# First pair's stores cut into transfers of one block row, with the planner's costs and priorities set anew

## The chip, the cores and the metric

The kernel runs on one core of a Trainium2 chip. The metric is device time in microseconds (us); before the change it was 748.63 us, the median of three runs (746.96 to 749.18).

## The reference

Eight batches of eight heads attend through 32 packed queries, and the result goes through a feed-forward layer with a GELU:

```python
def sm_attn(qq, kk, vv):                       # scale = 1/8
    s = scale * np.matmul(qq, kk.transpose(0, 1, 3, 2))
    a = np.exp(s - np.max(s, axis=-1, keepdims=True))
    a = a / (np.sum(a, axis=-1, keepdims=True) + 1e-09)
    return np.matmul(a, vv)

p_packed = sm_attn(p, k, v)                    # p: (8, 8, 32, 64); q, k, v: (8, 8, 576, 64)
out = sm_attn(q, p_packed, p_packed)           # (8, 8, 576, 64)
x = out.transpose(0, 2, 1, 3).reshape(4608, 512)
h = x @ w_in                                   # w_in: (512, 2048)
g = 0.5 * h * (1.0 + erf(h / np.sqrt(2.0)))
return g @ w_out                               # w_out: (2048, 512); result (4608, 512)
```

Everything is float32, and q, k and p are eight times larger than drawn.

## The kernel before

The batches go in four pairs. For each pair the attention ends in softmax weights `a2T` and packed values `pp`. The feed-forward layer of a pair is four units, one for each 512 columns of `w_in`; a unit has eight steps (`t8`), four for each batch of the pair, 32 steps a pair and 128 in all. In a unit `pp` is first multiplied by `w_in` (`wps`, L1118). A step then forms 128 hidden columns (`h`, L1184, or L1175 in the first unit), ScalarE takes the GELU into `graw` (L1206) and a rounded copy `g` (L1213), VectorE subtracts the copy from `graw` for the low part of `g` (L1215), and TensorE adds `g` times `w_out` into four output tiles `o` (L1236 to L1238, three products each; the third reads the low part). A ninth output tile of the unit, `o_edge`, takes the last 64 rows of both batches. VectorE adds the units' results into nine tiles `acc` of 128 rows by 512 (L1322), and after the fourth unit these are stored.

While a pair's steps run, the attention of the next pair runs beside them. `later_pair` (L1348) starts it when the step named in `LATER["from"]` comes up and the pair before has its scores. It loads p (L623), k and q (L563) and v (L612, L614). For pairs after the first, a k or q load is four transfers of 32 partitions, 144 KB each, and VectorE then transposes blocks (`kT`, `qT`, L581). The weights are decoded in the first pair (`wraw`, L1042 and L1046), kept in DRAM (`ws`, L1099) and read back as `w` in the later pairs (L1017). All transfers are issued by SyncE (SP), in one queue.

The first pair's rows lie in another order than the other pairs': an `acc` tile holds four blocks of 32 rows, and the rows of a block stand 18 apart in the output. So its store (L1337) writes through a view with the block outermost, `[4, 32, 512]`, or, for the tile that holds the end of one batch and the beginning of the other, two views with two blocks each. The other pairs store 128 rows that lie together (L1330).

The order of the instructions on each engine is written by a planner (`Order`), which runs the program twice: once without priorities, to get each operation's distance to the end (`tails_of`, with the factors `SLACK` and the offsets `EARLY` by kind and `SOONER` by name), and once with them, in which each engine and the transfer queue issue the ready operation of the highest priority. It reckons transfers with a number of issues and bytes: for each issue 0.5 us of the queue, and the bytes at one rate over one link (`issue`, L391 to L394). `MARGIN` and `DMA_MARGIN` are times by which it lets an operation begin later than what it reads is reckoned to be there, once the output steps have begun:

```python
if engine == DMA and self.steady:
    after += DMA_MARGIN
```

Here `engine` is that of the task's own operation just before (L332); an operation that waits for an event of another task has no such margin. While the first products are not there, TensorE is filled with products of zeros (`idle`, L1157). `FIRST["banks"]` says where the first pair's second scores are held in PSUM (L642), and `FIRST["turn"]` which engine copies the first pair's transposed k and q (L574).

Of the kernel before, what the change touches and what calls it, by code (L numbers as in the profile page):

```python
# [25 lines left out]
NB32 = S // 32  # L26
# [13 lines left out]
PE, ACT, DVE, POOL, DMA = "PE", "ACT", "DVE", "POOL", "DMA"  # L40
# [9 lines left out]


SLACK = {
    "batch0": 1.513,
    "batch1": 2.222,
    "attention": 2.432,
    "load0": 0.271,
    "load": 0.122,
    "w_in0": 3.279,
    "w_out0": 2.037,
    "w_in": 0.772,  # L60
    "w_out": 2.153,
    "packed_w_in": 1.479,
    "steps": 0.535,
}
EARLY = {
    "batch0": 15.0,
    "batch1": -9.3,
    "attention": 0.1,
    "load0": 0.7,
    "load": 21.2,  # L70
    "w_in0": 2.2,
    "w_out0": 6.9,
    "w_in": 0.2,
    "w_out": -8.0,
    "packed_w_in": -4.5,
    "steps": -3.6,
}

SOONER = {
    "0_0_0": 11.8,  # L80
    "0_0_1": 13.7,
    "0_1_0": -13.7,
    "0_1_1": -4.6,
    "0_2_0": -2.6,
    "0_3_0": -1.8,
    "0_4_0": -14.8,
    "0_5_0": 2.6,
    "chunk_0_0": -12.2,
    "chunk_0_1": 19.3,
    "chunk_1_0": -3.5,  # L90
    "chunk_1_1": -6.2,
    "softmax1": -18.6,
    "softmax1_0_0": 5.1,
    "softmax1_0_1": 20.8,
    "softmax1_1_0": -4.3,
    "softmax1_1_1": -36.8,
    "softmax2": -5.0,
    "softmax2_0_0": -11.8,
    "softmax2_0_1": -53.3,
    "softmax2_1_0": -17.3,  # L100
    "softmax2_1_1": -1.0,
    "wp_0_0": -19.7,
    "wp_0_1": -6.8,
    "wp_1_0": -5.1,
    "wp_1_1": -25.2,
}

MARGIN = 2.0

DMA_MARGIN = 3.0  # L110

STEP_MORE = 1.18

# [10 lines left out]
    "scores2": (21.8, 25.2),  # L124
    "softmax2": (27.3, 16.8, 34.3, 83.9),
    "weights2": (31.8, 53.8, 41.5, 53.2),
    "from": (2, 0, 2, 0),
    "groups1": ((0, 1, 2, 3),),
    "groups2": ((0, 1), (2, 3)),
}  # L130
# [19 lines left out]
    "groups2": ((0,), (1,), (2,), (3,)),  # L150
    "gpsimd": (1,),
    "copy": ('ACT', 'ACT', 'ACT', 'ACT'),
    "banks": (False, False, False, False),
    "small": (True, True, True, True),
    "together": True,

# [1 line left out]
        "decode": (0, 0, 0, 0, 0, 0, 0, 0), "rebias": (0, 0, 0, 0, 0, 0, 0, 0), "k": (0, 0, 0, 0), "q": (0, 0, 0, 0),  # L158
        "softmax1": (0, 0, 0, 0), "softmax2": (0, 0, 0, 0), "packed": (0, 0, 0, 0), "weights2": (0, 0, 0, 0),
    },  # L160
    "turn": {"k": ('DVE', 'ACT', 'ACT', 'ACT'), "q": ('ACT', 'DVE', 'ACT', 'ACT')},
}


# [98 lines left out]
class Order:  # L263
# [31 lines left out]
    def fire(self, event):  # L295
        if self.current:
            event.by = event.by | self.current.by
        event.count -= 1
        if event.count == 0:
            for fn in event.waiting:  # L300
                self.at(self.now, fn)

    def advance(self, task, value, engine):
# [16 lines left out]
        if isinstance(what, Op):  # L320
# [11 lines left out]
            if engine == DMA and self.steady:  # L332
                after += DMA_MARGIN
            first = 0 if self.dry else -self.tails[key] - SOONER.get(key, 0) - (SOONER.get(what.takes[0][1], 0) if what.takes else 0)
# [96 lines left out]
def packed_attention_gelu_ffn(ctx: ExitStack, tc: tile.TileContext, q, k, v, p, w_in, w_out, out):  # L431
# [12 lines left out]
    nc = tc.nc  # L444
# [14 lines left out]
    def plan(order):  # L459
# [801 lines left out]
        def output_steps():  # L1261
            for n in range(NU * 8):
                u, t8 = divmod(n, 8)
                j, c = divmod(t8, NC4)
                yield g_ready[n]
                if n % STEPS == LATER["from"][n // STEPS]:
                    fire(pair_started[n // STEPS])
                yield w_ready[u, 2 + c, 0]
                if order.dry:
                    yield from behind(n)  # L1270
                order.idle, order.steady = None, True
                g, w = gs.pop(n), wo[u, c]
                if c == 0:
                    ts = [None] * 4
                for i in range(4):
                    def product(*new, i=i):
                        cols = slice(i * P, (i + 1) * P)
                        three(new[0] if new else ts[i], (g[:, 0, cols], g[:, 1, cols]), w, c == 0, c == NC4 - 1)


                    new = () if c > 0 else (i,) if u > 0 else range(4) if i == 0 and FIRST["together"] else () if FIRST["together"] else (i,)
                    got = yield Op(
                        PE, 0.68, n, product, [(psum_o, f"o_{n}_{x}") for x in new], more=0 if i else STEP_MORE)
                    if new:
                        ts[i:i + len(new)] = got if len(new) > 1 else [got]
                    if c == NC4 - 1:
                        start(finish(u, i + 5 * j, ts[i], psum_o, n))
                gts.give(g)
                if j == 1 and c == NC4 - 1:
                    start(edge_output(u, n))  # L1290

        def edge_output(u, n):
            yield t4_ready[u]
            t = None
            for c in range(NC4):
                def product(*new):
                    g = t4[u, c]
                    three((new[0] if new else t)[:, 0], (g[:, 0], g[:, 1]), wo[u, c], c == 0, c == NC4 - 1)

                got = yield Op(PE, 0.68, n, product, [(wide, f"o_{u}_edge")] if c == 0 else [])  # L1300
                t = got if c == 0 else t
                t4s.give(t4.pop((u, c)))
                free_wo(u, c)
            yield from finish(u, 4, t, wide, n)
# [8 lines left out]
        def finish(u, i, t, ring_, n):  # L1313
            pr, f = divmod(u, NF)
            x = t[:, 0] if ring_ is wide else t
            if f == 0:
                acc[pr, i] = yield Op(ACT, 0.48, n, lambda a: nc.scalar.copy(a, x), [(accs, f"acc_{pr}_{i}")])
                ring_.give(t)
                fire(finished[u, i])
                return  # L1320
            a = acc[pr, i]
            yield Op(DVE, 0.6, n, lambda: nc.vector.tensor_tensor(a, x, a, ALU.add))  # L1322
            ring_.give(t)
            fire(finished[u, i])
            if f == NF - 1:
                r0 = pr * 2 * S + i * P

                def fn():
                    if pr:
                        nc.sync.dma_start(out[r0:r0 + P], a)  # L1330
                        return
                    for j in range(2):
                        rows = out[j * S:(j + 1) * S].rearrange("(x n) d -> n x d", n=NB32)
                        n0, n1 = max(4 * i - j * NB32, 0), min(4 * i + 4 - j * NB32, NB32)
                        if n0 < n1:
                            p0 = 32 * (n0 + j * NB32 - 4 * i)
                            nc.sync.dma_start(rows[n0:n1], a[p0:p0 + 32 * (n1 - n0)])  # L1337

                yield Op(DMA, (1 if pr or i != 4 else 2, 262e3), n, fn)
                fire(written[pr, i])  # L1340
                accs.give(a)

# [70 lines left out]
```

## Time and profile before

| what | value |
|---|---|
| median of three runs | 748.63 us |
| the profiled execution | 749.43 us |
| its span, first to last instruction | 747.7 us |
| mean granted clock of TensorE | 0.995 |
| TensorE busy | 729.9 us, 98% |
| VectorE, ScalarE, GpSimd busy | 392.7, 355.9, 149.7 us |
| transferred | 106.77 MB in 156049 packets, 143 GB/s over the span |

Busy time is the share of the span in which an engine's instructions run; a matmul's end is modelled. In the rows below PE is TensorE, DVE VectorE, ACT ScalarE, SPq the queue of SyncE, which issues the transfers. Lines of a timeline give the start, the time taken, engine, source line, operation, tiles (out<-in), shapes and count, and in brackets the idle time of the engine before, with what ended it.

### The profile page before, as it was taken

The page shows a single profiled execution, that of the slowest core. Times are in us where ns is not written, and L with a number is a line of the kernel's source. Part 1 is how long each engine was busy: PE and PEld are TensorE (multiplying, and loading weights), DVE is VectorE, ACT ScalarE, POOL GpSimd, SP SyncE. Part 2 cuts the span into 40 slices and gives each one's busy share as a digit, 9 for nine tenths or more (in the row PEclk, how much of TensorE's full clock was granted, in tenths as well). Part 3 has the DMA queues.
Part 4 walks back from the last instruction along what each step waited for, and adds up shares of the span by engine and source line. Part 5 has one row for each costly group of instructions (what it writes and reads, how often), then busy time and mean ns, then how long its engine had stood idle before and what let it go on. Part 6 is the DMA issues. An engine that isn't in the chain of part 4 may idle for free.

```text
span 747.7 us, 13236 instructions
## 1 busy us (share of the span) xinstructions
PE 729.9 (98%) x5313; PEld 588.6 (79%) x5313; DVE 392.7 (53%) x614; ACT 355.9 (48%) x601; POOL 149.7 (20%) x312
## 2 busy tenths in 40 slices
PE   8999999999999599999999999999999999999997
PEld 6677787787777478788777888788777888788886
DVE  5778858887783131652568341563458421333332
ACT  5788656856653233453445243363355243332331
POOL 2443444453411001101011110101011011101010
PEclk9999999999999999999999999999999999999999
DMA  9977997575516698332051999341241701303031
GB/s 303 370 257 124 250 205 227 157 250 199 170 59 198 102 181 218 40 130 83 23 179 59 276 167 198 76 117 67 64 167 59 240 1 59 112 29 113 1 112 71
DMA packets 156049, 106.77 MB, mean 143 GB/s; under 512 B 123732, under 2 KB 131924, under 8 KB 155988
## 3 DMA queue, kind: packets, MB, share of 16 engines
q1 hardware_dynamic: 155988, 105.93, 53.2%
q8 instruction: 42, 0.69, 0.4%
q14 instruction: 19, 0.16, 0.1%
HBM read 83.89 MB, written 22.02 MB: 142 GB/s over the span
## 4 chain that ended last, share of the span: by engine, by line
PE 87%; SPq 3%; DMA 3%; DVE 3%; ACT 2%; issue 1%; POOL 1%; ACTq 0%; DVEq 0%; POOLq 0%
PE h L1184 24%; PE o L1236 16%; PE o L1238 15%; PE o L1237 15%; PE wps L1118 4%; SPq L563 3%; PE o_edge L1236 2%; PE o_edge L1238 2%; PE o_edge L1237 2%; PE h L1175 2%; PE s L657 2%; DMA k<-in_k_dram 2%; DMA wraw<-in_moe_w_out_dram 1%; PE pp L799 1%; PE e1Tm L761 1%
## 5 line engine op out<-in xcount | busy, mean ns | idle before, releaser
L1184 PEld LDWEIGHTS h<-a2T,wp 128*128 128x128 f32 x1440 | 202.6, 188 | 14.7 <-issue 3.5
L1184 PE MATMUL h<-a2T,wp 128*128 128x288 f32 x1440 | 210.6, 295 | 0.4 <-DVE e L848 0.4
L1236 PE MATMUL o<-w,g 128*128 128x512 f32 x508 | 206.8, 407 | 2.0 <-DMA w<-ws 1.6
L1238 PE MATMUL o<-w,g 128*128 128x512 f32 x508 | 200.6, 395 | 8.1 <-DVE g L1215 8.1
L1206 ACT ACTIVATE graw<-h 128x576 f32<-128x576 f32 x127 | 82.8, 652 | 261.0 <-PE h L1184 241.4
L1237 PE MATMUL o<-w,g 128*128 128x512 f32 x508 | 199.5, 393 | 0.0
L1215 DVE TENSOR_TENSOR g<-graw,g 128x512 fp32r<-128x512 f32 x128 | 95.4, 746 | 195.4 <-ACT g L1213 195.2
L1226 POOL CAST t<-graw 128x64 fp32r<-128x64 f32 x128 | 35.2, 275 | 513.6 <-ACT graw L1206 393.1
L1236 PEld LDWEIGHTS o<-w,g 128*128 128x128 f32 x508 | 96.3, 190 | 44.1 <-issue 22.7
L1238 PEld LDWEIGHTS o<-w,g 128*128 128x128 f32 x508 | 96.1, 189 | 31.3 <-DVE g L1215 9.8
L1237 PEld LDWEIGHTS o<-w,g 128*128 128x128 f32 x508 | 96.1, 189 | 14.8
L1322 DVE TENSOR_TENSOR acc<-o,acc 128x512 f32<-128x512 f32 x96 | 63.4, 683 | 35.5 <-PE o L1238 35.5
L1213 ACT CAST g<-graw 128x512 fp32r<-128x512 f32 x128 | 79.4, 620 | 3.2
L1134 DVE TENSOR_TENSOR wp<-wps,wp 128x1024 fp32r<-128x1024 f32 x30 | 36.7, 1222 | 38.5 <-ACT wp L1129 38.5
L1129 ACT CAST wp<-wps 128x1024 fp32r<-128x1024 f32 x30 | 30.4, 1014 | 43.5 <-PE wps L1118 43.5
L1227 POOL TENSOR_TENSOR t<-graw,t 128x64 fp32r<-128x64 f32 x128 | 47.1, 368 | 10.2
L1118 PE MATMUL wps<-w,pp 64*32 64x512 f32 (+1 forms) x544 | 35.3, 576 | 0.0
L581 DVE STREAM_TRANSPOSE kT<-k 128x1152 f32<-128x1152 f32 x12 | 16.5, 1376 | 27.7 <-DMA k<-in_k_dram 27.6
L1157 PE MATMUL idle<-still 128*128 128x256 bf16 x201 | 27.2, 287 | 1.1 <-DVE still L455 1.1
L1088 POOL TENSOR_TENSOR wt<-wt 128x512 int32<-128x512 int32 x16 | 21.7, 1356 | 31.0 <-DVE wt L1066 25.4
L1080 POOL TENSOR_TENSOR w<-wt 128x512 int32<-128x512 int32 x16 | 22.7, 1423 | 22.4 <-DVE wt L1066 19.8
L1052 ACT ACTIVATE wt<-wraw 128x512 f32<-128x512 f32 x32 | 21.6, 675 | 9.8 <-DMA wraw<-in_moe_w_in_dram 6.1
(124 smaller groups left out, 668.6 us busy)
## 6 DMA issues: line engine op xcount, KB each, us to landing
w<-ws SPq DMA_DIRECT2D x72, 512.0 KB, 5.4
ws<-w SPq DMA_DIRECT2D x24, 512.0 KB, 5.7
out_dram<-acc SPq DMA_DIRECT2D x35, 256.0 KB, 3.3
wraw<-in_moe_w_in_dram SPq DMA_DIRECT2D x16, 512.0 KB, 3.7
wraw<-in_moe_w_out_dram SPq DMA_DIRECT2D x16, 512.0 KB, 5.1
v<-in_v_dram SPq DMA_DIRECT2D x16, 512.0 KB, 5.8
k<-in_k_dram SPq DMA_DIRECT2D x48, 144.0 KB, 5.2
q<-in_q_dram SPq DMA_DIRECT2D x48, 144.0 KB, 5.6
```

The source lines that it names most:

```text
L1118: nc.tensor.matmul(t[r0:r0 + 32, hh, :m], lhsT=pp[b][rows, hh, r0:r0 + 32], rhs=wi[u, hh][rows, g, cols], start=True, stop=True)
L1134: yield Op(DVE, 1.2, step, lambda: nc.vector.tensor_tensor(lo, x, hi.bitcast(F32), ALU.subtract))
L1184: nc.tensor.matmul(t[:, half, :HALF], lhsT=w[:, wpart, ch, fc], rhs=a2T[b, ch][:, apart, half * HALF:(half + 1) * HALF], start=ch == 0 and ...
L1206: lambda raw: nc.scalar.activation(raw.rearrange("p (a n) -> p a n", a=2), t[:, :, :HALF], AF.Gelu),
L1213: g = yield Op(ACT, 0.52, lead, lambda g: nc.scalar.copy(g[:, 0], main), [(gts, f"g_{n}")])
L1215: DVE, 0.6, lead, lambda: nc.vector.tensor_tensor(g[:, 1], main, g[:, 0].bitcast(F32), ALU.subtract),
L1226: nc.gpsimd.tensor_copy(dst[:, 0], side)
L1227: nc.gpsimd.tensor_tensor(dst[:, 1], side, dst[:, 0].bitcast(F32), ALU.subtract)
L1236: nc.tensor.matmul(t, lhsT=g[0], rhs=w[:, 0], start=first, stop=False)
L1237: nc.tensor.matmul(t, lhsT=g[0], rhs=w[:, 1], start=False, stop=False)
L1238: nc.tensor.matmul(t, lhsT=g[1], rhs=w[:, 0], start=False, stop=last)
L1322: yield Op(DVE, 0.6, n, lambda: nc.vector.tensor_tensor(a, x, a, ALU.add))
```

## The change

The store of the first pair goes out as one transfer for each block of 32 rows, four for a tile, and the planner reckons it with four issues instead of one. `DMA_MARGIN` goes from 3 to 1. The third entry of `LATER["from"]` goes from 2 to 0. `FIRST["banks"]` changes for two chunks and `FIRST["turn"]["k"][0]` from VectorE to ScalarE. `SLACK`, `EARLY` and `SOONER` get other values.

```diff
 SLACK = {
-    "batch0": 1.513,
+    "batch0": 1.805,
...
-    "w_out": 2.153,
-    "packed_w_in": 1.479,
+    "w_out": 1.189,
+    "packed_w_in": 1.103,
     "steps": 0.535,
 EARLY = {
...
-    "load": 21.2,
+    "load": 9.1,
...
 SOONER = {
...
-    "chunk_0_1": 19.3,
+    "chunk_0_1": 89.8,
...
-    "softmax1": -18.6,
+    "softmax1": 48.6,
...
-DMA_MARGIN = 3.0
+DMA_MARGIN = 1.0
...
-    "from": (2, 0, 2, 0),
+    "from": (2, 0, 0, 0),
...
-    "banks": (False, False, False, False),
+    "banks": (True, False, False, True),
...
-    "turn": {"k": ('DVE', 'ACT', 'ACT', 'ACT'), "q": ('ACT', 'DVE', 'ACT', 'ACT')},
+    "turn": {"k": ('ACT', 'ACT', 'ACT', 'ACT'), "q": ('ACT', 'DVE', 'ACT', 'ACT')},
...
-                    for j in range(2):
+                    for m in range(4 * i, 4 * i + 4):
+                        j, n0 = divmod(m, NB32)
                         rows = out[j * S:(j + 1) * S].rearrange("(x n) d -> n x d", n=NB32)
-                        n0, n1 = max(4 * i - j * NB32, 0), min(4 * i + 4 - j * NB32, NB32)
-                        if n0 < n1:
-                            p0 = 32 * (n0 + j * NB32 - 4 * i)
-                            nc.sync.dma_start(rows[n0:n1], a[p0:p0 + 32 * (n1 - n0)])
-
-                yield Op(DMA, (1 if pr or i != 4 else 2, 262e3), n, fn)
+                        nc.sync.dma_start(rows[n0], a[32 * (m - 4 * i):32 * (m - 4 * i) + 32])
+
+                yield Op(DMA, (1 if pr else 4, 262e3), n, fn)
```

## Rows read from the trace of the kernel before

**Rows 1.** The page's busy times, and its 40 slices in tenths.
```profile
PE 729.9 (98%) x5313; PEld 588.6 (79%) x5313; DVE 392.7 (53%) x614; ACT 355.9 (48%) x601; POOL 149.7 (20%) x312
...
PE   8999999999999599999999999999999999999997
```

**Rows 2.** PE's waits from 60 us on: total us, times, longest.
```profile
PE o L1238 <- DVE g L1215: 8.1, 2, 4.4
PE o L1236 <- DMA w<-ws: 1.6, 1, 1.6
```

**Rows 3.** PE in order of time, 225 to 270 us.
```profile
239.43 1.75 PE L1184 MATMUL h<-a2T,wp 128*128 128x288 f32 x12
...
242.83 0.47 PE L1236 MATMUL o<-w,g 128*128 128x512 f32 x1 [1.65 <-DMA w<-ws]
...
251.61 0.80 PE L1238 MATMUL o<-w,g 128*128 128x512 f32 x1 [3.73 <-DVE g L1215]
...
262.10 0.79 PE L1238 MATMUL o<-w,g 128*128 128x512 f32 x1 [4.39 <-DVE g L1215]
...
265.89 1.72 PE L1184 MATMUL h<-a2T,wp 128*128 128x288 f32 x12
```

**Rows 4.** PE in order of time, 423 to 435 us.
```profile
425.08 1.75 PE L1184 MATMUL h<-a2T,wp 128*128 128x288 f32 x12
...
429.40 1.75 PE L1184 MATMUL h<-a2T,wp 128*128 128x288 f32 x12
```

**Rows 5.** Stretches: us; busy PE, PEld, DVE, ACT, POOL; clock; DMA share; GB/s.
```profile
250.00:255.00 5.00, 3.39 (x8) 2.75 (x9) 1.55 (x2) 1.69 (x4) 0.00 (x0) 0.66 0.34 76
...
260.00:265.00 5.00, 2.90 (x7) 2.32 (x8) 2.46 (x3) 0.00 (x0) 0.00 (x0) 0.67 1.17 129
```

**Rows 6.** VectorE in order of time, 225 to 270 us.
```profile
249.60 1.38 DVE L581 STREAM_TRANSPOSE kT<-k 128x1152 f32<-128x1152 f32 x1 [10.62 <-DMA k<-in_k_dram]
...
260.09 1.38 DVE L581 STREAM_TRANSPOSE kT<-k 128x1152 f32<-128x1152 f32 x1 [8.54 <-DMA k<-in_k_dram]
```

**Rows 7.** SP's queue in order of time, 215 to 270 us.
```profile
225.30 4.28 SPq L1337 DMA_DIRECT2D out_dram<-acc  x4
229.67 4.14 SPq L1017 DMA_DIRECT2D w<-ws  x3
233.87 12.94 SPq L563 DMA_DIRECT2D k<-in_k_dram  x4
...
248.07 16.95 SPq L563 DMA_DIRECT2D k<-in_k_dram  x12
```

**Rows 8.** The chain that ended last, 215 to 270 us: start, us, what.
```profile
234.49 7.70 SPq L563
```

**Rows 9.** Transfers, 206 to 217 us: packets, MB, share of 16 engines.
```profile
q1 hardware_dynamic: 435, 0.87, 25.1%
```

**Rows 10.** Transfers, 411 to 415 us.
```profile
q1 hardware_dynamic: 292, 0.98, 86.9%
```

**Rows 11.** SP's queue in order of time, 385 to 460 us.
```profile
417.73 21.37 SPq L563 DMA_DIRECT2D k<-in_k_dram  x16
```

**Rows 12.** VectorE in order of time, 385 to 450 us.
```profile
429.54 1.38 DVE L581 STREAM_TRANSPOSE kT<-k 128x1152 f32<-128x1152 f32 x1 [0.61 <-DMA k<-in_k_dram]
```

**Rows 13.** Issues of two lines: ns min/median/max, first and last start us.
```profile
L1337 SPq DMA_DIRECT2D out_dram<-acc x10: 527/554/1057, 204.9 to 247.5; - x10
...
L623 SPq DMA_DIRECT2D p<-in_p_dram x16: 378/450/978, 0.7 to 474.4; - x16
```

**Rows 14.** ScalarE's waits, 0 to 60 us.
```profile
ACT wt L1052 <- DMA wraw<-in_moe_w_in_dram: 6.1, 3, 3.9
```

**Rows 15.** Groups of instructions on PE, 0 to 60 us: busy us, mean ns.
```profile
L1157 PE MATMUL idle<-still 128*128 128x256 bf16 x201 | 27.2, 287 | 1.1 <-DVE still L455 1.1
```

**Rows 16.** The chain that ended last, 0 to 62 us.
```profile
18.97 11.09 DMA wraw<-in_moe_w_out_dram
```

**Rows 17.** Stretches, columns as in Rows 5.
```profile
60.00:238.00 178.00, 177.68 (x1279) 140.71 (x1279) 134.43 (x206) 112.25 (x191) 71.06 (x100) 1.00 0.74 190
```

More of the change, by code (lines that the diff above doesn't have):

```diff
@@ L52 @@
 SLACK = {
-    "batch0": 1.513,
[L54 to L60, printed above, removed]
-    "w_out": 2.153,
-    "packed_w_in": 1.479,
+    "batch0": 1.805,
+    "batch1": 2.067,
+    "attention": 2.371,
+    "load0": 0.169,
+    "load": 0.137,
+    "w_in0": 3.068,
+    "w_out0": 1.984,
+    "w_in": 0.766,
+    "w_out": 1.189,
+    "packed_w_in": 1.103,
     "steps": 0.535,
@@ L65 @@
 EARLY = {
[L66 to L69, printed above, removed]
-    "load": 21.2,
[L71 to L74, printed above, removed]
+    "batch0": 14.5,
+    "batch1": -9.1,
+    "attention": -0.5,
+    "load0": -0.0,
+    "load": 9.1,
+    "w_in0": 3.4,
+    "w_out0": 7.3,
+    "w_in": -0.4,
+    "w_out": -4.9,
     "packed_w_in": -4.5,
@@ L79 @@
 SOONER = {
[L80 to L88, printed above, removed]
-    "chunk_0_1": 19.3,
-    "chunk_1_0": -3.5,
-    "chunk_1_1": -6.2,
-    "softmax1": -18.6,
[L93 to L105, printed above, removed]
+    "0_0_0": 13.7,
+    "0_0_1": 16.8,
+    "0_1_0": -11.6,
+    "0_1_1": -4.7,
+    "0_2_0": -3.1,
+    "0_3_0": -1.5,
+    "0_4_0": -28.2,
+    "0_5_0": -0.7,
+    "chunk_0_0": -19.0,
+    "chunk_0_1": 89.8,
+    "chunk_1_0": -3.5,
+    "chunk_1_1": -5.4,
+    "softmax1": 48.6,
+    "softmax1_0_0": 40.2,
+    "softmax1_0_1": 36.3,
+    "softmax1_1_0": -5.1,
+    "softmax1_1_1": -10.6,
+    "softmax2": -48.0,
+    "softmax2_0_0": -26.1,
+    "softmax2_0_1": -48.7,
+    "softmax2_1_0": -69.0,
+    "softmax2_1_1": -47.5,
+    "wp_0_0": -28.4,
+    "wp_0_1": 17.6,
+    "wp_1_0": -21.6,
+    "wp_1_1": -51.8,
 }
 MARGIN = 2.0
-DMA_MARGIN = 3.0
+DMA_MARGIN = 1.0
 STEP_MORE = 1.18
```

## The prediction

> **What bounds the kernel now.** I read the head of the page first: TensorE (PE) is busy 98% of the span, and its row of tenths shows 9 in every slice but the first, the last and the fourteenth, near 250 us, which shows 5 [rows 1]. So outside the start only time in which PE stands still can be won. Second, PE's list of waits after 60 us: three events of size in 687 us, 8.1 us in two waits of `o` products for VectorE's subtraction `g` (L1215), and 1.6 us in one for a reloaded weight `w` [rows 2]. Third, PE in order of time shows all three in one place, at 242.83, 251.61 and 262.10 us [rows 3]. What the place costs I take from the beat of the steps, not from the waits: the hidden product `h` begins at 239.43 and, three steps later, at 265.89, which is 26.46 us [rows 3]; where the next pair passes the same point two `h` lie 4.32 us apart [rows 4], so three steps take 12.97. Lost: 13.49 us. The three waits are 9.77 of it [rows 3]; the other 3.72 us are products at the lower of the two clock levels, 1.2 GHz, which is granted for part of the five microseconds behind each of the two longer stalls: the mean share there is 0.66 and 0.67 [rows 5].
>
> Who was late? VectorE runs in the written order, and before each late `g` stands a transpose `kT` (L581) that waited 10.62 and 8.54 us for a k transfer [rows 6]. These are the k loads of the third pair. SyncE's (SP's) queue shows why they are late: four output stores of the first pair at 225.30, three weight reloads that take 4.14 us to issue, then the first four k transfers, 12.94 us to issue [rows 7]; in the chain of waits one of these issues alone lasts 7.70 us [rows 8]. Other issues of the same kind take 3.94 us and less there, so I take it that this one is held by what is ahead of it in the engines. What is ahead is seen where the first pair's stores run alone, 206 to 217 us: the transfer engines are at 25.1%, a quarter of sixteen engines, with 0.87 MB in 11 us, 79 GB/s [rows 9]. The stores of the second pair, contiguous rows (L1330), run at 86.9% with 0.98 MB in 4 us [rows 10]. A first-pair store thus keeps some four of sixteen engines busy (my reading of 25.1%), about three to four times as long as an even spread would.
>
> **The change part by part.** Stores (L1337). Nine tiles go out as 36 transfers of 64 KB instead of ten. At 79 GB/s [rows 9] a burst of four tiles, 1.05 MB, needs 13.3 us on its quarter of the engines; at the second pair's 0.98 MB in 4 us [rows 10] it would need 4.3. So the queue behind a burst comes free about 9 us sooner. What the k loads do behind evenly spread stores the trace shows one pair later: sixteen k transfers begin at 417.73 and take 21.37 us to issue [rows 11] against 233.87 to 265.02 in two stretches [rows 7]; the first `kT` there waits 0.61 us [rows 12] and PE loses nothing. In the beat of the steps the two places differ by 185.65 us (425.08 less 239.43 [rows 3, 4]), so 417.73 stands for 232.08, 1.8 us ahead of 233.87: the k loads began almost equally late in both, and what differs in kind is the stores ahead.
>
> The price is issue time. A first-pair store now takes 554 ns on SP, and a 64 KB transfer (p) a median of 450 ns, 378 at the least and 978 at the most [rows 13]. Four tiles become 16 issues: 6.0 us at the least, 7.2 at the median, 15.6 at the most, where the burst of four took 4.28 [rows 7]. I take 7.2, the row of nearest size: SP is 2.9 us later. Behind the stores in SP's queue stand the three `w` and then k; PE asks for the late `w` at about 241 us [rows 3], and with three issues at the 378 ns of a short transfer [rows 13] they leave SP by 225.30 + 7.2 + 1.1 = 233.6 us, no later than now (233.81 [rows 7]) and with free engines behind them. I put the extra issue time at 0, hidden behind those 7 us, and use its bounds in a rival: at 15.6 the `w` leave at 242, after PE asks.
>
> Room behind a landing (`DMA_MARGIN`, 3 to 1). In the code it acts on the operation that directly follows a transfer in its own task: up to 24 decodes of weights that come once the output steps have begun, and six p transposes. It takes no wait out and puts none in; it sets only where in ScalarE's and PE's order they stand. kT and the products that read `w` wait through events and never had it. Its cost is at most 2 us of waiting per place if loads land as late as planned before. ScalarE waited for these loads 6.1 us in three waits, 3.9 the longest, all before 60 us [rows 14]; later none. The cover: VectorE's late `g` waited 10.62 us and PE lost 3.73, or 8.54 and 4.39 [rows 3, 6], so 4 to 7 us of delay between `h` and `o` cost nothing, and 2 is under that. Nor can less room win anything where PE has no gap. Bounds 0 and, for the p transposes that PE itself reads, 6 times 2; I take 0.
>
> Third-to-fourth-pair start (`from`, third entry 2 to 0). The fourth pair's whole attention, with 16 k, 16 q, 4 p and 8 v transfers, is released two steps, 8.6 us, earlier. SP's queue passes no store with them that holds a quarter of the engines: the second pair's stores are the contiguous kind [rows 10]. GpSimd's queue has nothing of it. I take 0; the bad end is a rival below, the good end is 0 as PE has no gap at 425 us.
>
> The start. New turns, psum banks and priorities reorder the first 60 us and neither add nor drop a product there; three copies of k move from VectorE to ScalarE. PE's fill products, 27.2 us [rows 15], are the ceiling of a gain; the longest wait of the chain there, 11.09 us for a `w_out` tile that lands at 30.06 [rows 16], is my bound for a loss. Between these I take 0, with 3 us either way from the row of 3.9 us [rows 14]. After 60 us the other priorities move work beside a PE that is busy 177.68 of 178 us [rows 17] and, behind the stalls, has no wait worth naming to the end [rows 2]: 0.
>
> Sum: the profiled execution took 749.43 us (span 747.7 and 1.7 around it) and is 0.80 above the median of 748.63. 749.43 - 13.49 = 735.94, or 735.1 from the median. I predict 735.5.
>
> A rule against the change: the Trainium skill, DMA: Bandwidth & Descriptors, section "Rules for kernel authors", advises against cutting a transfer into partition parts, since the parts share the same engines and small ones are mostly overhead. By it the sum would be 748.6, which is rival (c). The same page's section on why a DMA increments its semaphore by 16 says that the slowest dimension sets how many engines work; the old store's is 4, the new one's 32. The 25.1% agrees with the second [rows 9], and I follow the row.
>
> **The rivals.** (a) Issue time becomes the bound. At 0.98 us an issue SP is 8 us later or more; a `w` or a k is late again. For: in the present queue issues do stretch to 7.70 us [rows 8]. Against: the thing that stretched them goes. Price: one stall like the second, 4.39 us, with half of the 3.72 for the clock, so 6.2 of the 13.5 stay: 735.1 + 6.2 = 741.3.
>
> (b) Slower: the early release is what makes `kT` too early. The third pair has the release at 0 and stalls, the fourth has 2 and does not; after the change both have 0, and VectorE in the fourth pair too would stand in `kT` while `g` waits. For: that pairing, and that VectorE reaches the first `kT` at 238.98 in the third pair [rows 6] but at 428.93 in the fourth [rows 12], which on the other scale is 243.28, a step later. Against: reached a step sooner, the fourth pair's `kT` would wait 0.61 + 4.32 = 4.9 us, and 4 to 7 are covered; and the k issues of the stalled pair are only 1.8 us later, so the 10.62 us are not made by the release. Price: of 13.49 only the `w` wait, 1.65, goes, and 11.84 comes at about 425 us: 748.6 - 1.65 + 11.84 = 758.8. It decides once k lands more than about 4 us after VectorE has reached `kT`.
>
> (c) The split does nothing, since four transfers of 64 KB hold the engines as long as one of 256: 748.6. Against: 25.1% beside 86.9%.
>
> **How the numbers follow.** Stall gone: 0.63, range 731.5 to 738.5 (3 us of the start, and half a us of the two bases). (a) 0.20, 738.5 to 746. (b) 0.11. (c) 0.06. A measurement of this kernel tells some 0.3% from no change, 2.2 us. Faster by more: 0.63 + 0.20 = 0.83; same 0.06; slower 0.11. The range 731 to 746 holds the first two cases and a little below the first, for a start that gains more.
>
> **What would show it.** Right: the row of tenths full at the fourteenth slice; PE's waits for L1215 gone; no L563 issue above some 3 us near 240; a transfer share well over 25% at 206 us; the k loads of the third pair issued in some 21 us. Wrong: `kT` waits of over 5 us near 240 or 420 (b); long L1337 stretches with a PE wait for `w` behind them (a); fill products of the start that grow or shrink by more than 3 us (the start).

## The result and the profile after

The changed kernel took 736.93 us in the median of four runs (735.98 to 739.95) against 748.9 us before: a ratio of 0.9851, 95% interval 0.9817 to 0.9885. The profiled execution took 735.98 us with a span of 734.2, 13.5 us under that of before. The forecast was 735.5.

First the page's row of tenths for PE, which answers to [rows 1]. The hole in the fourteenth slice is gone; the seventh and the sixteenth slice, near 117 and 279 us, are a little short, where two of the waits below stand.

```profile
PE   8999998999999998999999999999999999999998
```

The fill products of the first 60 us answer to [rows 15] (count, busy us, mean ns):

```profile
L1157 PE MATMUL idle<-still 128*128 128x256 bf16 x151 | 21.0, 287 | 1.1 <-DVE still L455 1.1
```

PE's waits from 60 us on answer to [rows 2]: total us, times, longest. The wait for VectorE's `g` falls from 8.1 to 1.9 us, that for a reloaded `w` is 2.3 instead of 1.6 and stands elsewhere, at 279 us, and two waits for ScalarE, both in the first pair, are new.

```profile
PE o L1236 <- DMA w<-ws: 2.3, 1, 2.3
PE o L1238 <- DVE g L1215: 1.9, 3, 1.2
PE h L1184 <- ACT e L717: 1.6, 1, 1.6
PE h L1184 <- ACT pp L817: 0.9, 1, 0.9
```

The place of the old stall, in PE's order of time (lines left out are marked). The first and the last line are the two `h` that stand at 239.43 and 265.89 in [rows 3]. Three steps now take 14.53 us, 1.56 more than the undisturbed 12.97; before it was 13.49 more.

```profile
235.17 1.75 PE L1184 MATMUL h<-a2T,wp 128*128 128x288 f32 x12
...
247.28 0.50 PE L1238 MATMUL o<-w,g 128*128 128x512 f32 x1 [1.25 <-DVE g L1215]
...
249.70 1.75 PE L1184 MATMUL h<-a2T,wp 128*128 128x288 f32 x12
```

SP's queue there answers to [rows 7]: 20 small stores, all ahead of the weights, and the 16 k transfers in one stretch of 21.09 us, like the next pair's before [rows 11].

```profile
221.04 11.26 SPq L1335 DMA_DIRECT2D out_dram<-acc  x20
232.39 1.82 SPq L1017 DMA_DIRECT2D w<-ws  x4
234.26 21.09 SPq L563 DMA_DIRECT2D k<-in_k_dram  x16
```

VectorE's first transpose still waits, but it now stands a step later (the `g` before it is that of the `h` at 235.17), and of its 6.24 us PE feels 1.25.

```profile
238.34 0.69 DVE L1215 TENSOR_TENSOR g<-graw,g 128x512 fp32r<-128x512 f32 x1 [3.62 <-ACT g L1213]
245.27 1.38 DVE L581 STREAM_TRANSPOSE kT<-k 128x1152 f32<-128x1152 f32 x1 [6.24 <-DMA k<-in_k_dram]
```

So between these two profiles the 13.5 us come in three parts: the first of the two `h` is 4.26 us sooner (235.17 against 239.43), which the start and the first pair gave (other profiles of the same two orders show less, by the table below); the place itself gives 11.93; and 2.7 are lost behind it (the second `h` is 16.19 us sooner, the end 13.5). The loss is mostly the 2.3 us wait for `w`, at 279 us.

### The profile page after: what moved, and what is told of

Same layout as the page of the kernel before. It is cut to its first block, busy times and chain, and to the rows that moved or that the text cites. A ratio compares the mean times of both kernels' runs of the same rounds, so it can differ in the third digit from the quotient of the medians.

```text
span 734.2 us, 13174 instructions
## 1 busy us (share of the span) xinstructions
PE 720.6 (98%) x5263; PEld 580.7 (79%) x5263; DVE 388.5 (53%) x611; ACT 357.1 (49%) x604; POOL 151.9 (21%) x312
## 4 chain that ended last, share of the span: by engine, by line
PE 82%; DMA 7%; SPq 3%; ACT 3%; DVE 3%; issue 1%; DVEq 0%; ACTq 0%
PE h L1184 23%; PE o L1236 14%; PE o L1238 14%; PE o L1237 13%; PE wps L1118 4%; DMA wraw<-in_moe_w_in_dram 4%; SPq L563 3%; PE h L1175 2%; PE o_edge L1236 2%; PE o_edge L1238 2%; PE o_edge L1237 2%; PE pp L799 2%; DMA wraw<-in_moe_w_out_dram 1%; PE s L657 1%; DMA k<-in_k_dram 1%
## 5 line engine op out<-in xcount | busy, mean ns | idle before, releaser
L1236 PE MATMUL o<-w,g 128*128 128x512 f32 x508 | 205.1, 404 | 2.3 <-DMA w<-ws 2.3
L1238 PE MATMUL o<-w,g 128*128 128x512 f32 x508 | 199.1, 392 | 1.9 <-DVE g L1215 1.9
L1215 DVE TENSOR_TENSOR g<-graw,g 128x512 fp32r<-128x512 f32 x128 | 95.1, 743 | 181.8 <-ACT g L1213 181.3
L1226 POOL CAST t<-graw 128x64 fp32r<-128x64 f32 x128 | 37.2, 291 | 500.1 <-ACT graw L1206 393.4
L1236 PEld LDWEIGHTS o<-w,g 128*128 128x128 f32 x508 | 95.4, 188 | 40.3 <-issue 22.5
L1238 PEld LDWEIGHTS o<-w,g 128*128 128x128 f32 x508 | 95.4, 188 | 24.9 <-DVE g L1215 3.8
L1080 POOL TENSOR_TENSOR w<-wt 128x512 int32<-128x512 int32 x16 | 21.0, 1314 | 23.7 <-DVE wt L1066 9.2
L1060 DVE TENSOR_SCALAR wt<-wt 128x512 f32<-128x512 f32 x32 | 17.2, 538 | 15.5 <-ACT wt L1052 15.5
```

Source lines behind the costliest of these rows:

```text
L1215: DVE, 0.6, lead, lambda: nc.vector.tensor_tensor(g[:, 1], main, g[:, 0].bitcast(F32), ALU.subtract),
L1226: nc.gpsimd.tensor_copy(dst[:, 0], side)
L1236: nc.tensor.matmul(t, lhsT=g[0], rhs=w[:, 0], start=first, stop=False)
L1238: nc.tensor.matmul(t, lhsT=g[1], rhs=w[:, 0], start=False, stop=last)
```

## The experiments

To see what happens between, this table has the start of the output product with which a step begins, counted out of the 1728 products of L1236 to L1238 (13.5 a step), in us from the start of the span; step 128 stands for the last one. "Room" is `DMA_MARGIN`, "split" the store cut into one transfer for each block.

```
kernel                       step 0     16      32      36      64     128
before                        55.10  141.79  230.78  263.97  416.42  743.48
after                         47.95  135.67  226.52  248.31  402.66  730.16
after, a second profile       48.03  137.54  228.57  250.13  403.32  729.99
split alone                   53.98  140.66  229.59  254.84  406.78  733.85
two blocks                    53.97  140.64  229.58  274.26  426.68  753.76
split, from GpSimd            53.88  140.54  229.54  249.81  401.74  728.82
after, old stores             47.88  137.14  228.34  257.37  411.61  738.29
after, from GpSimd            47.77  137.75  228.80  249.07  400.60  727.49
priorities alone              48.02  140.35  230.91  265.04  418.03  745.59
room 1 alone                  53.99  141.86  236.41  268.91  422.46  750.18
split, reckoned as four       54.24  140.10  238.27  258.54  412.12  739.20
after, room 3                 47.99  140.03  230.05  251.04  407.35  736.67
after, fourth pair at 2       47.99  138.47  229.40  251.67  406.69  733.37
```

Four rows have the order of before on the computing engines (before, split alone, two blocks, split from GpSimd), and five have that of the changed kernel up to step 64 (after, its second profile, old stores, from GpSimd, fourth pair at 2). At step 32 the four lie between 229.5 and 230.8 us, the five between 226.5 and 229.4. The means are 229.9 and 228.3. So one order differs by up to 2.9 us between executions, and the two profiles that the section above compares are the latest of the four and the earliest of the five.

**The split alone.** The kernel before, the written order of the computing engines unchanged.

```diff
...
-                        if n0 < n1:
-                            p0 = 32 * (n0 + j * NB32 - 4 * i)
-                            nc.sync.dma_start(rows[n0:n1], a[p0:p0 + 32 * (n1 - n0)])
+                        nc.sync.dma_start(rows[n0], a[32 * (m - 4 * i):32 * (m - 4 * i) + 32])
```

> The kernel before with the first pair's stores as four transfers of one block each, reckoned by the planner as before, so that every engine's order stays what it was. Theory (a store whose slowest dimension is 4 works on four of sixteen engines, and that backlog makes the stall of 13.5 us near 240 us): the stores run at well over 25% transfer share, no k issue over 3 us near 240, the first kT there waits some 7 instead of 10.6 us, PE loses 1 to 3 us in place of 13.5; 736 to 739 us. Rival (the gain comes from the new order of the first 60 us, not from the stores): 748.6, stall unchanged. Rival (four small transfers hold queue and engines as long): 747 to 750.

Measured: 739.35 us, ratio 0.9868 (0.9853 to 0.9882), just over the 736 to 739 expected. PE in order of time between the same two `h`: 17.99 us, so 5.02 lost in place of 13.49, and not the 1 to 3 expected.

```profile
238.24 1.75 PE L1184 MATMUL h<-a2T,wp 128*128 128x288 f32 x12
...
247.19 0.50 PE L1238 MATMUL o<-w,g 128*128 128x512 f32 x1 [2.41 <-DVE g L1215]
...
253.79 0.50 PE L1238 MATMUL o<-w,g 128*128 128x512 f32 x1 [2.00 <-DVE g L1215]
...
256.23 1.75 PE L1184 MATMUL h<-a2T,wp 128*128 128x288 f32 x12
```

The two waits are 4.41 us of the 5.02. The granted clock stays at 1.00 behind them (244 to 254 us), so most of the 3.72 us that products at the lower level had cost is gone too.

SP's queue shows what is left. The burst of four tiles issues for 8.90 us where it took 4.28 [rows 7], so the first four k transfers begin at 234.72, no sooner than before, and the first `kT` waits 7.40 us.

```profile
224.32 8.90 SPq L1335 DMA_DIRECT2D out_dram<-acc  x16
233.32 1.35 SPq L1017 DMA_DIRECT2D w<-ws  x3
234.72 7.46 SPq L563 DMA_DIRECT2D k<-in_k_dram  x4
```

```profile
245.19 1.38 DVE L581 STREAM_TRANSPOSE kT<-k 128x1152 f32<-128x1152 f32 x1 [7.40 <-DMA k<-in_k_dram]
```

The transfer share from 206 to 217 us is 32.4% (first line), but the last of these stores has landed before 214. From 206 to 213 us alone (second line) it is 48.1%, at 0.81 MB. It does not reach the 86.9% of [rows 10], since the issues now pace the stores: 1.05 MB in 8.6 to 8.9 us.

```profile
q1 hardware_dynamic: 625, 0.85, 32.4%
q1 hardware_dynamic: 586, 0.81, 48.1%
```

The split takes 8.5 us out of the stall, with its longer issue time already paid. Both rivals of this run are out.

**Two blocks a transfer.** If the engines are set by the slowest (outermost) dimension, two blocks are worse than four.

```diff
...
-                            nc.sync.dma_start(rows[n0:n1], a[p0:p0 + 32 * (n1 - n0)])
+                        nc.sync.dma_start(rows[n0:n0 + 2], a[p0:p0 + 64])
```

> The kernel before with each first-pair store as two transfers of two blocks, 64 rows and 128 KB each, order as before. If the slowest dimension sets the number of engines, each works on two: transfer share near 13% where the stores run alone, a burst of four tiles needs some 26 us, the k loads come 10 us later still, 755 to 768 us. Rival (the number or the size of the transfers matters, not their slowest dimension): between the two kernels or like before, 742 to 749 us, share at 25% or over.

Measured: 760.27 us, ratio 1.0148 (1.0133 to 1.0163), slower than before, although the transfers are smaller and more. Transfers from 206 to 217 us (packets, MB, share of sixteen engines), the row that answers to [rows 9]: 12.7% is two of sixteen, as 25.1% was four. Counted in the traces' packet records, two packets of 2 KB rows are under way at once for most of this burst, four for most of that of before, and up to sixteen with the split.

```profile
q1 hardware_dynamic: 233, 0.46, 12.7%
```

The second burst holds SP's queue for 16.83 us, and the k transfers begin 11.39 us later than before:

```profile
224.10 16.83 SPq L1336 DMA_DIRECT2D out_dram<-acc  x8
245.26 11.89 SPq L563 DMA_DIRECT2D k<-in_k_dram  x4
```

PE waits 13.4 us for a `w` and twice behind `kT`:

```profile
PE o L1236 <- DMA w<-ws: 13.4, 1, 13.4
PE o L1238 <- DVE g L1215: 7.1, 2, 5.6
```

**Small stores from another queue.** The split alone, with the 36 stores issued by GpSimd.

```diff
-                        nc.sync.dma_start(rows[n0], a[32 * (m - 4 * i):32 * (m - 4 * i) + 32])
+                        nc.gpsimd.dma_start(rows[n0], a[32 * (m - 4 * i):32 * (m - 4 * i) + 32])
```

> The kernel before with the split stores, order as before, and the split stores issued from GpSimd's queue instead of SP's. With the split alone SP issued a burst of four tiles for 8.9 us, the w and the k loads stood behind it, and PE still lost 4.4 us in two waits behind kT. Theory (what is left of the stall is issue time on SP): the k loads begin some 5 us sooner, the kT waits fall under 4 us, PE loses under 1 us there: 734 to 736 us. Rival (what is left is the rate of the k transfers themselves): the waits stay within 1 us of 4.4, 738 to 740.

Measured: 735.05 us, ratio 0.9808 (0.9783 to 0.9834). SP's k transfers begin at 229.48, the first `kT` waits 3.98 us, and between the same two `h` lie 12.98 us: 0.01 lost.

```profile
238.19 1.75 PE L1184 MATMUL h<-a2T,wp 128*128 128x288 f32 x12
...
251.17 1.75 PE L1184 MATMUL h<-a2T,wp 128*128 128x288 f32 x12
```

```profile
229.48 21.70 SPq L563 DMA_DIRECT2D k<-in_k_dram  x16
```

```profile
241.72 1.38 DVE L581 STREAM_TRANSPOSE kT<-k 128x1152 f32<-128x1152 f32 x1 [3.98 <-DMA k<-in_k_dram]
```

The k transfers were not quicker here, only sooner: from the first issue to the first `kT` pass 12.24 us, against 10.47 with the split alone, but they begin 5.24 us earlier. The stores also stand in another transfer queue of the page here, but that did not speed the loads. So the rival, their rate, is out. The stall of 13.49 us is thus wholly the stores': the split takes 8.5 of it, by the engines that the old stores kept, and the other 5.0 go with the issue time in SP's queue, which the split itself raises. The old stores from GpSimd were not run, so what the engines alone cost is not shown.

**The old store in the changed kernel.** The order of the changed kernel, the stores as before, `rows[n0:n1]`, still reckoned as four issues.

```diff
...
-                        nc.sync.dma_start(rows[n0], a[32 * (m - 4 * i):32 * (m - 4 * i) + 32])
+                            nc.sync.dma_start(rows[n0:n1], a[p0:p0 + 32 * (n1 - n0)])
```

> The changed kernel with the first pair's stores as one transfer of four blocks again (two of two blocks for the tile across batches), still reckoned as four issues, so that the order is that of the changed kernel. Theory: the stall near 235 to 260 us comes back with 8 to 12 us, less the 4.3 us that the changed start holds: 744 to 748 us. Rival (start): within 1 us of the changed kernel, 736 to 738.

Measured: 744.86 us, ratio to before 0.9944 (0.9922 to 0.9966). The stall is back, as waits for `w`, since here the weights stand behind six old stores.

```profile
PE o L1236 <- DMA w<-ws: 9.3, 2, 6.6
PE h L1184 <- ACT e L717: 1.5, 1, 1.5
PE o L1238 <- DVE g L1215: 1.3, 1, 1.3
```

**The priorities alone.** The kernel before with the new `SLACK`, `EARLY`, `SOONER`, banks and turn.

```diff
...
-    "banks": (False, False, False, False),
+    "banks": (True, False, False, True),
...
-    "turn": {"k": ('DVE', 'ACT', 'ACT', 'ACT'), "q": ('ACT', 'DVE', 'ACT', 'ACT')},
+    "turn": {"k": ('ACT', 'ACT', 'ACT', 'ACT'), "q": ('ACT', 'DVE', 'ACT', 'ACT')},
```

> The kernel before with the changed kernel's priorities, psum banks and turn alone; stores, room behind a landing and release of the fourth pair as before. Theory (the start gives some 4 us, the stores the rest): output steps begin about 7 us sooner than 55.10 us, of which some 4 to 5 are left at step 32; the stall near 240 us stays at about 13: 743 to 746 us. Rival (all from the stores): 748 to 750, start unchanged.

Measured: 751.78 us, ratio 1.0045 (1.0027 to 1.0064): slower, where 743 to 746 were expected. The steps begin 7.1 us sooner, but by step 32 the lead is gone (table). PE's waits from 60 to 230 us name seven of some size, where before had one of 0.3:

```profile
PE h L1184 <- DVE wp L1134: 2.0, 1, 2.0
PE s L657 <- ACT e1T L774: 1.2, 1, 1.2
PE h L1184 <- ACT graw L1206: 0.9, 1, 0.9
```

**Room 1 alone, and room 3 in the changed kernel.** The edit in the kernel before; in the changed kernel its reverse.

```diff
-DMA_MARGIN = 3.0
+DMA_MARGIN = 1.0
```

> The kernel before with DMA_MARGIN 1 alone. Theory (2 us less room are covered by the time between h and o): ScalarE waits for weight loads in the first pair by up to 2 us a time, PE loses under 1 us, the stall near 240 us stays: 747 to 750 us. Rival (less room lets ScalarE stand in front of the GELU): PE loses 2 to 6 us between 60 and 230 us, 751 to 755. Rival (less room packs the first pair better): the steps up to step 32 come 2 to 5 us sooner, 744 to 747.

Measured: 755.73 us, ratio 1.0104 (1.0075 to 1.0132). The steps lose 6.7 us between step 0 and 32 (table: from 1.1 ahead to 5.6 behind), and PE's longest wait between 60 and 230 us is for ScalarE:

```profile
PE h L1184 <- ACT graw L1206: 2.6, 1, 2.6
```

That is the first rival's mechanism, and a little over its 751 to 755. The named waits make up some 4 of the 6.7; where the rest goes stays open.

> The changed kernel with DMA_MARGIN 3 again. The changed priorities with room 3 and the old stores began the steps 7 us sooner and had lost all of it by step 28; the changed kernel kept 4.3. If the room of 1 is what kept it: 739 to 743 us, the start's lead gone by step 28. Rival (the room does nothing, the lead is kept by the stores' reckoning): within 1 us of the changed kernel, 736 to 738, with ScalarE's waits for weight loads after 60 us gone.

Measured: 742.4 us, ratio to before 0.9926 (0.9898 to 0.9955), and 5.5 above the changed kernel (4.7 above its second run, below). So the same step from 3 to 1 costs in one plan and wins in the other. By the table 3.5 of the loss stand at step 32 against the first profile of the changed kernel, 1.5 against the second, and the rest before step 128. The rival's sign did not come either: of ScalarE's waits for weights 9.1 us are left between 60 and 230 us, 14.2 in the changed kernel.

**The split, reckoned as four issues.** The split alone with the planner's new cost.

```diff
-                yield Op(DMA, (1 if pr or i != 4 else 2, 262e3), n, fn)
+                yield Op(DMA, (1 if pr else 4, 262e3), n, fn)
```

> The kernel before with the split stores reckoned as four issues each; the planner may now order the rest anew. The split alone left 4.4 us of waits for kT near 244 and 251 us, since its stores issue for 8.6 us where the planner reckoned 2. Theory (with the true number of issues kT is written later behind the stores): those waits shrink to 1 us or so, 734 to 737 us. Rival (the planner's reckoning of the stores changes nothing that counts): 738 to 740, as with the split alone.

Measured: 746.63 us, ratio 0.9972 (0.9951 to 0.9993), 7.3 us above the split alone, where 734 to 737 were expected. The place does what was expected, no wait of PE for `g` is left, and from step 32 to 36 it is 12.9 us quicker than before. But the new order loses 8.4 us before step 32 (from 0.9 ahead to 7.5 behind), 4.7 of it in one wait near 181 us, where VectorE does decode work ahead of the transpose that frees a psum bank:

```profile
PE s L657 <- DVE e L848: 4.7, 1, 4.7
```

**The release of the fourth pair.**

```diff
-    "from": (2, 0, 0, 0),
+    "from": (2, 0, 2, 0),
```

> The changed kernel with the fourth pair released at its old step. In the changed kernel the second kT of the fourth pair waits 5.04 us and PE loses 0.7 us there. Theory (the early release costs that and no more): 735.5 to 737, no PE wait near 420 us. Rival (the early release costs several us in other places): under 735. Rival (it wins some): over 738.

Measured: 739.0 us (737.84 to 740.5), ratio to before 0.9878 (0.9849 to 0.9906). That is over the 735.5 to 737 expected, but its order differs from the changed kernel's only behind step 64, and 2.9 us stand at step 32 already: one order's spread between executions. From step 64 on it takes 326.7 us, 0.8 less than the first profile of the changed kernel, which loses 0.7 at 422 us (its `h` at 419.97 and 425.00 lie 5.03 us apart, not 4.32). But the second profile of that kernel, with the release at 0, also takes 326.7 us from step 64 on, and its `h` there lie 4.35 apart. The second `kT` of the fourth pair, in the two:

```profile
420.58 1.38 DVE L581 STREAM_TRANSPOSE kT<-k 128x1152 f32<-128x1152 f32 x1 [5.04 <-DMA k<-in_k_dram]
420.57 1.38 DVE L581 STREAM_TRANSPOSE kT<-k 128x1152 f32<-128x1152 f32 x1 [4.63 <-DMA k<-in_k_dram]
```

So the early release costs between nothing and 0.7 us, and neither the time of the whole nor one profile of the stretch tells which.

**The changed kernel again, and two versions of it.**

> The changed kernel once more, on the same chip as the other three, so that they are compared with it and not with another day's runs: 736 to 738 us. A kernel that differs from it only behind step 64 came to 739.0, and by the steps 2.9 us of that stood before step 32, where both have the same order; if that is the spread of one kernel, this one shows a start 1 to 3 us later than in its first profile.

Measured: 737.72 us (735.85 to 740.75), ratio 0.9848 (0.9812 to 0.9883). Its profile has step 32 2.05 us later and the end 0.17 sooner than the first.

> The changed kernel with its split stores issued from GpSimd. Theory (issue time on SP): the 1.25 us wait of o behind kT near 246 us goes and nothing else, 1 to 2 us under the changed kernel run beside it. Rival (the issues on GpSimd hold up the copies t, which the edge products read): PE waits before o_edge, 1 us or more over the changed kernel.

The edit is that of the stores from GpSimd, in the changed kernel. Measured: 733.54 us (732.86 to 733.99), ratio to before 0.9787 (0.9761 to 0.9813), and 4.2 under the changed kernel run beside it, where 1 to 2 were expected. More went than the theory had: the `w` wait of 2.3 us near 279 too. SP's k and q loads are through earlier, and the weights behind them.

This run also shows what all the planner's changes are worth together once the stall is out of the way: with the stores from GpSimd the order of before takes 735.05 us and the changed order 733.54, 1.5 less.

For the last run the planner reckons the k and q loads of the later pairs slower.

```diff
-            cost, fn = ((1, 590e3), rows) if bt.b < 2 else ((4, 1640e3, 2), blocks)
+            cost, fn = ((1, 590e3), rows) if bt.b < 2 else ((4, 2090e3, 2), blocks)
```

> The changed kernel with the k and q loads reckoned at 2090e3 instead of 1640e3 bytes a load, which at the planner's rate is 5.4 us, what 21.09 us for four loads show. Theory (the kT and w waits that are left come from loads reckoned too fast): kT waits under 3 us, the w wait of 2.3 us near 276 us gone, 732 to 735 us. Rival (a new reckoning orders the whole first pair anew and loses there what it gains, as room and reckoning did alone): 737 to 745.

Measured: 732.93 us (732.86 to 733.25), ratio to before 0.978 (0.9749 to 0.981), the lowest median, 0.6 us under that with the stores from GpSimd. No wait for `w` is left, and the `g` waits of 1.9 us are 0.7:

```profile
PE h L1184 <- ACT graw L1206: 2.2, 3, 1.5
PE h L1184 <- ACT pp L817: 1.2, 2, 0.9
PE h L1184 <- DVE wp L1134: 1.0, 1, 1.0
PE o L1238 <- DVE g L1215: 0.7, 1, 0.7
```

The two edits were not run together.

## Why the prediction was right, step by step

- **The stall and its cause.** Right, in size too: 13.49 us was read from the beat of the steps, and with the stores spread and out of SP's queue 0.01 of it is left. Four of sixteen engines was a reading of 25.1%; the run at 12.7% with two blocks shows that the count of blocks sets it. This agrees with the Trainium skill, DMA: Bandwidth & Descriptors, section "Why a DMA increments its semaphore by 16 and not by 1". The rule in the section "Rules for kernel authors" of that page of the Trainium skill, against cutting a transfer into partition parts, does not hold here, where the uncut one has a slowest dimension of 4.
- **Issue time put at 0.** This term was mis-sized. In the order of before it costs 5.0 us (17.99 against 12.98 between the same two `h`), close to the 6.2 of rival (a), and the split alone, at 739.35, lies in that rival's range. I had looked at what PE asks of `w` and found 7 us of room (5.4 of which such a load takes to land, by the page of before), but not at `kT`, whose room was already overdrawn: the k loads began where they had before. In the changed kernel the planner reckons with four issues and writes `kT` a step later, so 1.56 is left. A burst of four tiles took 8.6 to 9.4 us to issue, not the 7.2 that I took: the median issue, 0.42 us, is under my 0.45, but the longest are 1.19 us (split alone) and 1.69 (changed kernel). The 4.3 us in which evenly spread stores were to move a burst was misread: in the stretch of [rows 10] two weight loads of 512 KB run beside the stores, so it shows no rate of stores alone. The 2 KB packets of a burst span 13.4 us before, as reckoned, and 8.7 with the split alone, so the engines come free some 5 us sooner and not 9.
- **The start put at 0.** Mis-sized the other way: the steps begin 7.15 us sooner, 6.0 against the other three profiles of the order of before, and the fill products shrink from 27.2 to 21.0 us, both outside the 3 us allowed. Most of that is lost again in the first pair. Of the lead 1.5 us reach step 32 by the means of the four and the five profiles, 4.26 in the pair shown above.
- **Luck.** What the sum had at 0 nearly cancels: some 1.5 us won at the start, against some 1.5 for the rest of the stall and 0.4 to 2.3 lost from step 36 on (the two profiles of the changed kernel against that of before). That 735.5 came so near to 736.93 is owed to this as well as to the main term.
- **The signs.** The full row of tenths, the k loads in some 21 us and a share well over 25% came. PE's waits for L1215 did not go (1.9 us), and one k issue still lasts 4.39 us in the changed kernel, over the 3 allowed. Two signs of being wrong came as well: `kT` waits over 5 us (6.24 and 5.04), without the stall of (b), and the shrunken fill products. These limits were set too tight for what they were to tell.
- **Room put at 0, from a cover of 4 to 7 us.** The cover is real (`kT`'s 6.24 us cost PE 1.25), but it was the wrong question. A margin moves the planner's whole first pair: alone it cost 6.7 us by the medians, in the changed kernel its undoing cost 5.5 (4.7 against the second run). The loss lies in my bounds of 0 to 12, though PE lost it in waits for ScalarE and not for p; the gain I had ruled out, because PE had no gap to win, and overlooked that a plan with other priorities has gaps of its own.
- **The release put at 0, and rival (b).** The mechanism is there and small. The argument had the fourth pair's first `kT` wait 4.9 us; it waits 2.73, as the k loads begin sooner too (402.55 against 417.73), and the second 5.04. PE loses 0.7 there in one profile and nothing in the other, so the cover of 4 to 7 us held.
- **What the parts are worth** does not add: the split -10.0, the priorities +2.5, the room +6.7 (by the medians, each against the kernel before run beside it); the whole change is -12.0. Of these only the split wins by itself; the release was not run alone. Together, with the stall out of the way, the planner's changes win 1.5 (735.05 to 733.54).

## What to carry to other kernels

Read a transfer's engines from its share when it runs alone, over a window that ends when it ends. A store whose outermost dimension is 2 or 4 is worth cutting into transfers whose outermost dimension is long (32 here), even if that takes four of them; then ask in which queue the added issues stand and who is behind them. On an engine that runs in the written order a transpose that waits for a load holds everything behind it, so a late load costs where its reader is written, not where the load is. And a constant of a planner has no price of its own: try it with the others, and compare the same steps of profiles rather than totals, with more than one profile of each kernel: here one order differed by up to 2.9 us at the same step.

## What the runs showed that was not expected

What stores on few engines cost shows in the issue times on SP. Four k transfers took 12.94 us to issue behind stores that held four engines [rows 7], 11.89 behind stores that held two, whose own eight issues had already taken 16.83, and 7.46 behind spread ones. It does not go to nothing: behind spread stores too one k issue takes some 4 us (4.39 in the changed kernel), and why is not shown. The Trainium skill, DMA: Bandwidth & Descriptors, section "Issuing engines are not separate DMA queues", says that issuing from another engine saves only issue time, which is usually small beside the transfer; here that saving was 4.3 us (739.35 to 735.05), because the queue it was taken from held the loads that PE was waiting for. GpSimd's issues took 496 to 675 ns each.
